# Talking-heads attention and mixture of experts: all four batches in float32, v as the stationary operand, products ordered by array form

## The chip, the cores and the metric

One NeuronCore of a Trainium2 chip. The metric is device microseconds of one execution; lower is better. The profile is of one execution of the program, taken by the hardware profiler. The engines are TensorE (PE; its weight loads PEld), VectorE (DVE), ScalarE (ACT), GpSimd (POOL) and SyncE (SP), which issues most DMAs.

## What is computed

Attention over 4 batches, 12 heads, 448 rows, head size 64, with the heads mixed by a 12 x 12 matrix before the softmax and by another after it; then each of the 1792 rows (12 heads x 64 = 768 values) goes through one of 8 experts, chosen by the largest cosine logit.

```python
scores = scale * np.matmul(q, k.transpose(0, 1, 3, 2))
scores = np.einsum('bhij,hg->bgij', scores, w_pre)
attn = exp(scores - max); attn = attn / (sum + 1e-9)
attn = np.einsum('bhij,hg->bgij', attn, w_post)
x = np.matmul(attn, v)              # 1792 rows of 768
e = argmax(normed(x) @ normed(expert_emb).T / tau)
out = gate * (relu(x @ w1[e]) @ w2[e])
```

## The kernel before

**Row tiles and groups.** A batch's 448 rows are cut into four row tiles of 110, 110, 110 and 120 rows, 16 in all. A row tile is worked through in groups of 10 rows: 10 rows x 12 heads fill 120 partitions, so that the mixing of heads is a product with a 120-row block matrix. There are 11 or 12 groups in a row tile, 180 in the program.

**One row tile.** `emit_qk` (`emit_qk32` in batch 0) makes the scores of two heads at a time into the PSUM tiles p_s; they are copied to SBUF (shl) and written to a DRAM tile `sdr`. `emit_read` reads them back in three chunks of up to four groups with the rows regrouped (g). For each group `emit_pre` mixes the heads (p_p), `emit_max` takes the row maxima, `emit_exp` the exponentials and their sums, `emit_r` the reciprocal and, on GpSimd, the post-mixing matrix scaled by it (wr); `emit_post` mixes the heads and turns the result at once (p_m: three products of 128 columns of e, and two halves of 64 for the rest), and it is copied into a whole row tile of attention weights. `emit_av` multiplies them with v for the row tile before; `emit_xc`, `emit_xt`, `emit_xtc`, `emit_lg` copy x, turn it, and take the eight logits. x goes to the DRAM tensor x_tok, from which the experts' part gathers rows.

**Two number formats.** In batch 0 scores and pre-mixing are float32; a head's scores come from a q tile whose other 64 rows are zeros, so that all 128 rows of the array are used for one head. In batches 1 to 3 q, k, the scores and w_pre are pairs of float16 pieces (hi and lo): `prep(b)` loads the batch's q, k and v twice, once for the largest magnitude and once for the pieces; `pow2` takes the maximum over the partitions with GpSimd's partition_all_reduce and forms powers of two from it; ScalarE makes the hi pieces, GpSimd or VectorE the lo pieces, and `stack` copies q and k pieces from SBUF to SBUF so that the two pieces lie in the two halves of the partitions. In all batches the attention weights (ahi, alo) and v (vh, vl) are float16 pieces, and `emit_av` takes three products for each of four key blocks of a head, with the weights stationary (128 x 128) and 64 columns of v moving.

**What sets the order.** Every engine's program is in the order in which the code emits it. The main loop runs over the 180 groups; `PLAN` and the lists MX1, MX2, ST1 and others give the group of the row tile in which each piece of side work is emitted. Within a turn gi of the loop: reciprocal of gi - 1, the copies left from the turn before (late_a, late_v), exponential of gi, pre-mixing of gi + 2, scores of a later row tile, post-mixing of gi - 2, logits, transposes, products with v, reads, maxima of gi + 2, prepared parts. Scores run about one row tile ahead. `s_p` has 2 buffers of three heads' score pieces, `g_p` 4 chunks. PSUM: two banks for p_s, three for p_p, two for p_m, one (xb) for x, its transposes and logits. At the start the first row tile's scores go from SBUF straight into `g_first`, without DRAM.

The functions that the change touches:

Of the kernel before, what the change touches and what calls it, by code (L numbers as in the profile page):

```python
# [26 lines left out]
AW = 42 * 120  # L27
NTL = 4 * B
NE = 12
CAP = 256  # L30
CCH = 8
MAXO = 12
NRAW = 9
MX1 = (3, 3, 2, 2, 3, 4, 4, 10, 6, 6, 9, 10, 18, 19, 21, 23, 22, 22)
H1 = 14
V0 = 8
HV = 4
VL = 3
ST1 = (8, 15)
ST2 = 13  # L40
RO = 5
MX2 = (-18, -17, -15, -15, -16, -15, -14, -12, -13, -15, -14, -10, -9, -10, -9, -9, -7, -7)
NW = 5
NWARM = 7
SUMS = ((0, 4), (2, 5), (3, 5), (3, 4), (0, 6), (3, 6), (1, 4), (2, 4), (0, 5))
LEAD = 4
RD0 = (4, 5, 6)
RD = (5, 7, 10)
Q0P = (4, 8, 9, 9)
# [5 lines left out]
QPH3 = 10  # L55
NS = 18
TP = 8
QPH = 10
PLAN = {
    "small": {  # L60
        "qk": (0, 2, 4, 6, 8, 10),
        "av": (3, 3, 3, 4, 5, 6, 6, 7, 9, 9, 10, 10),
        "xc": (5, 8, 11),
        "xt": (7, 8, 11),
        "xtc": (8, 11, 13),
        "sq": 13,
        "lg": (8, 12, 13),
    },
    "large": {
        "qk": (0, 2, 4, 8, 9, 10),  # L70
        "av": (2, 3, 3, 3, 5, 5, 6, 8, 10, 10, 10, 10),
        "xc": (5, 9, 11),
        "xt": (5, 9, 13),
        "xtc": (6, 11, 14),
        "sq": 16,
        "lg": (9, 13, 15),
    },
    "ahead": {
        "av": (4, 4, 4, 4, 6, 6, 7, 7, 8, 9, 9, 9),
        "xc": (5, 8, 10),  # L80
        "xt": (7, 9, 10),
        "xtc": (9, 10, 12),
        "sq": 13,
        "lg": (9, 12, 13),
    },
    "last": {
        "av": (2, 2, 3, 3, 4, 4, 5, 5, 6, 6, 6, 7),
        "xc": (4, 6, 8),
        "xt": (4, 7, 8),
        "xtc": (5, 8, 11),  # L90
        "sq": 11,
    },
}
# [5 lines left out]
def talking_heads_moe(  # L99
# [3 lines left out]
    q0: bass.AP,  # L103
# [3 lines left out]
    wpre32: bass.AP,  # L107
# [24 lines left out]
    wpre_sb = const.tile([120, 64], F32, name="wpre_sb")  # L132
    wpre32_sb = const.tile([120, 128], F32, name="wpre32_sb")
# [49 lines left out]
    with tc.manual_schedule():  # L183
# [6 lines left out]
        big = ax.enter_context(tc.tile_pool(name="big", bufs=1))  # L190
        g_p = ax.enter_context(tc.tile_pool(name="g", bufs=4))
# [10 lines left out]
        def open_tmp():  # L202

            nonlocal tmp_p
            gx.close()
            tmp_p = bx.enter_context(tc.tile_pool(name="tmp", bufs=1, side="right"))
# [649 lines left out]
        for n in range(2, 6):  # L856
            load_k(n)
# [660 lines left out]
```

## Time and profile before

| | us |
|---|---|
| median of 3 runs (1039.89 to 1054.26) | 1046.91 |
| the profiled execution | 1048.54 |
| its span, first to last instruction | 1046.7 |
| TensorE busy, VectorE, ScalarE, GpSimd | 895.5, 612.7, 552.2, 253.7 |
| mean granted TensorE clock, share of 2.4 GHz | 0.902 |
| DMA moved | 189.61 MB |

The sum of busy times says little here, since the program has three stages: the start-up to the first exponential, the 180 groups, and the experts. It is read stage by stage.

### The profile page before, as it was taken

The numbers are of one execution on the slowest core, as the hardware profiler recorded it, in microseconds if no ns is written. First come the engines' busy times: TensorE is split into PE (matmuls) and PEld (weight loads), VectorE is DVE, ScalarE is ACT, GpSimd is POOL, SyncE is SP. The second block draws the span as 40 slices with busy tenths as digits, with TensorE's granted clock in tenths as the row PEclk, the third lists the DMA queues.
The fourth block names the chain that finished last, engine by engine and source line by source line (L and its number), as shares of the span: only waits on it lengthen the run. The fifth ranks groups of instructions, "written<-read, shape, count | busy, mean of one in ns | idle before, by whom it ended". The sixth has DMA issues, their size and how long they took to land. (4 is left out here: it accounts for less than half of the span.)

```text
span 1046.7 us, 20350 instructions
## 1 busy us (share of the span) xinstructions
PE 895.5 (86%) x7532; PEld 690.9 (66%) x7532; DVE 612.7 (59%) x1559; ACT 552.2 (53%) x1168; POOL 253.7 (24%) x526
## 2 busy tenths in 40 slices
PE   7295969849979586989999989897799999999995
PEld 3162746526645454656666656676699999999994
DVE  1063546536876353768657767465467865565562
ACT  4073745526857263867657756463254543454351
POOL 3021423003533111545112212223142012111110
PEclk9597988878989696999989989798999999999998
DMA  8785785855878655668756655722587667765671
GB/s 156 156 212 154 210 253 141 221 132 169 231 209 246 180 99 130 198 190 241 213 109 186 188 146 110 226 74 81 86 298 227 222 197 225 238 213 194 196 244 45
DMA packets 99246, 189.61 MB, mean 181 GB/s; under 512 B 9809, under 2 KB 68377, under 8 KB 99144
## 3 DMA queue, kind: packets, MB, share of 16 engines
q1 hardware_dynamic: 95591, 175.75, 61.1%
q0 software_dynamic: 3552, 12.53, 3.6%
q8 instruction: 60, 0.98, 0.4%
q14 instruction: 43, 0.34, 0.1%
HBM read 130.27 MB, written 48.54 MB: 171 GB/s over the span
## 5 line engine op out<-in xcount | busy, mean ns | idle before, releaser
L621 PEld LDWEIGHTS p_m<-wr,e 128*128 128x128 f32 x1080 | 152.1, 210 | 112.3 <-POOL wr L612 62.1
L621 PE MATMUL p_m<-wr,e 128*128 128x120 f32 x1080 | 181.2, 309 | 51.0 <-POOL wr L612 51.0
L632 ACT ACTIVATE ahi<-p_m 128x420 f16<-128x420 f32 x180 | 97.9, 544 | 126.1 <-PE p_m L623 125.1
L635 DVE TENSOR_TENSOR alo<-p_m,ahi 128x420 f16<-128x420 f32 x180 | 106.3, 590 | 97.1 <-ACT ahi L632 96.5
L612 POOL TENSOR_TENSOR wr<-wpost_sb,r 128x120 f32<-128x120 f32 x180 | 69.9, 388 | 373.1 <-DVE r L609 279.4
L592 DVE TENSOR_REDUCE mn<-p_p 128x1 f32<-128x448 f32 x180 | 110.1, 612 | 69.0 <-PE p_p L583 43.2
L954 ACT ACTIVATE wh<-raw_w 128x768 fp32r<-128x768 f32 (+2 forms) x132 | 113.1, 903 | 45.3 <-DMA raw_w<-w 37.6
L955 DVE TENSOR_TENSOR wl<-raw_w,wh 128x768 fp32r<-128x768 f32 (+2 forms) x128 | 126.9, 1030 | 15.4 <-ACT wh L954 15.3
L523 DVE SCALAR_TENSOR_TENSOR shl<-p_s,shl 110x448 f16<-110x448 f32 (+1 forms) x144 | 83.3, 617 | 53.6 <-ACT shl L520 53.4
L520 ACT ACTIVATE shl<-p_s 110x448 f16<-110x448 f32 (+1 forms) x144 | 70.9, 542 | 74.8 <-DMA sdr<-shl 38.3
L600 ACT ACTIVATE e<-p_p,mn,uo 128x448 f32<-128x448 f32 x135 | 97.7, 724 | 0.0
L651 PEld LDWEIGHTS <-ahi 128*128 128x128 f16 (+1 forms) x1536 | 87.9, 101 | 13.6
L1304 PE MATMUL p_h<-xh,wh 128*128 128x256 f32 x336 | 96.8, 288 | 0.0
L1304 PE MATMUL p_h<-xh,wl 128*128 128x256 f32 x336 | 95.1, 283 | 0.0
L1304 PE MATMUL p_h<-xl,wh 128*128 128x256 f32 x336 | 95.1, 283 | 0.0
L651 PE MATMUL xb<-vh,ahi 128*128 128x64 f16 x720 | 94.0, 201 | 0.0
L651 PE MATMUL xb<-vh,alo 128*128 128x64 f16 x720 | 93.3, 198 | 0.0
L651 PE MATMUL xb<-vl,ahi 128*128 128x64 f16 x720 | 93.3, 198 | 0.0
L1056 POOL DMA_INDIRECT out<-o,idx_s x17 | 23.6, 1388 | 218.6 <-DVE o L1324 183.4
L1322 PE MATMUL p_o<-wh,hh 128*128 128x384 f32 x224 | 75.6, 338 | 0.0
L1306 ACT ACTIVATE hh<-p_h 128x512 fp32r<-128x512 f32 x28 | 16.7, 598 | 111.2 <-PE p_h L1304 91.6
L1322 PE MATMUL p_o<-wl,hh 128*128 128x384 f32 x224 | 74.9, 334 | 0.0
(269 smaller groups left out, 1898.2 us busy)
## 6 DMA issues: line engine op xcount, KB each, us to landing
g<-sdr SPq DMA_DIRECT2D x34, 840.0 KB
raw_w<-w SPq DMA_DIRECT2D x54, 512.0 KB
raw_w<-w SPq DMA_DIRECT2D x72, 384.0 KB
sdr<-shl SPq DMA_DIRECT2D x42, 577.5 KB
sdr<-shl SPq DMA_DIRECT2D x16, 630.0 KB
raw<-vP SPq DMA_DIRECT2D x36, 256.0 KB
raw<-qT SPq DMA_DIRECT2D x36, 224.0 KB
raw<-kT SPq DMA_DIRECT2D x36, 224.0 KB
```

The source lines that it names most:

```text
L520: A.activation(out=sb[:n, j, :], in_=p[:n, :S], func=ACTF.Copy, scale=2.0 ** -19)
L523: V.scalar_tensor_tensor(out=sb[:n, j + 1, :], in0=p[:n, :S], scalar=2.0 ** -19, in1=sb[:n, j, :], op0=ALU.mult, op1=ALU.subtract)
L592: V.tensor_reduce(out=mn[:, 0:1], in_=p[:, :S], op=ALU.max, axis=AX.X, negate=True)
L600: A.activation(out=e, in_=p[:, :S], func=ACTF.Exp, scale=exp_scale(gi)[:, 0:1], bias=mn[:, 0:1], accum_out=mn[:, 1:2])
L621: T.matmul(p[:, jt * 120:jt * 120 + 120], e[:, jt * 128:jt * 128 + 128], wr, start=True, stop=True)
L632: A.activation(out=dst(ahi), in_=src, func=ACTF.Copy)
L635: V.tensor_tensor(out=dst(alo), in0=src, in1=dst(ahi), op=ALU.subtract)
L651: T.matmul(p[:, g % 4 * D:(g % 4 + 1) * D], a[t % 2][r, a0:a0 + 128], v[r, c0:c0 + D], start=(jt == 0 and k == 0), stop=(jt == 3 and k == 2))
L954: A.activation(out=h[:, c], in_=r[:, c], func=ACTF.Copy)
L955: lo = lambda: eng.tensor_tensor(out=l[:, c], in0=r[:, c], in1=h[:, c].bitcast(F32), op=ALU.subtract)
L1304: T.matmul(p[:, f], lt[:, c], rt_[:, k], start=(k == 0 and i == 0), stop=(k == KD - 1 and i == 2))
L1322: T.matmul(p[:, :384], lt[:, k, c], rt_[:, m], start=(k == 0 and i == 0), stop=(k == KF - 1 and i == 2))
```

## The change

The float16 pieces, `prep`, `pow2` and the lists that placed them are gone. All batches go the way of batch 0, in float32, with these differences. The scores of two heads come from rows 0 to 63 and 64 to 127 of q and k as they are loaded (no zeros), into two PSUM banks. The first row tile's scores go through DRAM too. All score copies of the loop are on VectorE, all copies of p_m on ScalarE. In `emit_av` v is stationary: for a pair of heads, one product of 128 x 128 and six of 128 x 64, whose results lie turned (features on partitions), so the copy of that gives the logits' operand, and x is turned back by transposes. In a turn the products stand in the order of their form: pre-mixing, transposes, logits, first part of post-mixing, first product with v (128 x 128); second part of post-mixing and the six products with v (128 rows x 64 columns); scores (64 rows x 128 columns).

```diff
-        def prep(b):
...
-        def pow2(mx, n, top, tag):
...
-            G_.partition_all_reduce(out_ap=ar, in_ap=mx, channels=128, reduce_op=bass_isa.ReduceOp.max)
...
+        qk_p = bx.enter_context(tc.tile_pool(name="qk", bufs=2, side="right"))
+        s_p = bx.enter_context(tc.tile_pool(name="s", bufs=6, side="right"))
...
+        def emit_qk(t, a, banks, engs):
...
+            for u in range(2):
+                own = slice(64 * u, 64 * u + 64)
+                T.matmul(ps[u][:n, :S], q_sb[b][own, a, c0:c0 + n], k_sb[b][own, a, :], start=True, stop=True)
...
+                    if engs[u] is A:
+                        A.activation(out=sb[:n, u], in_=ps[u][:n, :S], func=ACTF.Copy, scale=0.125)
                     else:
...
+                        V.tensor_scalar(out=sb[:n, u], in0=ps[u][:n, :S], scalar1=0.125, scalar2=None, op0=ALU.mult)
+                qk_done[0] += 1
+                Y.dma_start(out=sdr[t][2 * a:2 * a + 2].rearrange("h i s -> i h s"), in_=sb[:n])
...
-            for w, st_, sp_ in ((wh, True, False), (wl, False, True)) if t > 3 else ():
-                for u in range(2):
-                    T.matmul(p[64 * u:64 * u + 64, :S], w, gt[t, 2 * m // CCH][:, 2 * m % CCH + u, :], start=st_, stop=sp_)
+            T.matmul(p[:, :S], wpre_sb, gt[t, m // CCH][:, m % CCH, :], start=True, stop=True)
...
-            G_.tensor_tensor(out=mn[:, 0:1], in0=mn[:, 0:1], in1=exp_scale(gi), op=ALU.mult)
...
-                V.tensor_tensor(out=dst(alo), in0=src, in1=dst(ahi), op=ALU.subtract)
...
+        def emit_av(t, a, p=None, c=None):
...
+            T.matmul(p[:, c:c + n], v[:, 768 + v0:768 + v0 + 128], w[:, (36 + a) * 120:(36 + a) * 120 + n],
+                     start=True, stop=False, skip_group_check=True)
+            yield
+            for jt in range(3):
+                for u in range(2):
+                    x0 = (jt * H + a + 6 * u) * 120
+                    d0 = jt * 256 + v0 + 64 * u
+                    T.matmul(p[64 * u:64 * u + 64, c:c + n], v[:, d0:d0 + 64], w[:, x0:x0 + n],
+                             start=False, stop=(jt == 2), skip_group_check=True)
+            yield
...
+        for ch in range(3):
+            emit_read(0, ch)
+        for j in range(3):
+            load_v(0, j)
...
+            for f in halves:
+                next(f)
+
+            want = min(6 * NTL, 6 * (t + 1) + QPH // 2 + sum(q <= pos for q in QK_AT))
+            if qk_n < want:
+                tq, a = divmod(qk_n, 6)
+                late_v.append(emit_qk(tq, a, banks[:2], (V, V)))
```

How the order moves, on TensorE in the middle of a batch: before, from the last pre-mixing product of a turn (p_p) over the scores of two heads (p_s) and the post-mixing (p_m) to the first products with v (xb); an x and a number counts products that follow each other.

```order
L586 LDWEIGHTS wl
L586 MATMUL p_p<-g,wl 64x448
L511 LDWEIGHTS qs
L511 MATMUL p_s<-kh,qs 110x448
...
L514 LDWEIGHTS qs
L514 MATMUL p_s<-tl,qs 110x448
...
L621 MATMUL p_m<-wr,e 128x120 x3
L623 MATMUL p_m<-wr,e 64x60 x2
L651 LDWEIGHTS ahi_132
L651 MATMUL xb<-vh,ahi_132 128x64
L651 LDWEIGHTS alo_134
L651 MATMUL xb<-vh,alo_134 128x64
```

And now, a whole turn of row tile 1 and the head of the next, which has a pair of transposes (L354):

```order
L270 MATMUL p_p<-g,wpre_sb 128x448
L303 MATMUL p_m<-wr,e 128x120 x3
L327 MATMUL xb<-att_126,v 128x110
L306 MATMUL p_m<-wr,e 64x60 x2
L334 MATMUL xb<-att_126,v 64x110 x6
L240 MATMUL p_s<-k,q 120x448 x2
L270 MATMUL p_p<-g,wpre_sb 128x448
L354 MATMUL xb<-id_sb,xT 110x128 x2
```

What moved: the scores stand behind everything else of the turn, the two parts of post-mixing are pulled apart by the first product with v, and twelve products with v for each head have become seven for a pair.

On GpSimd in row tile 2, before: the scaled post-mixing matrix (wr) of each group, the scaling of the maxima (mn), the lo pieces (tt, tl), and between them the maximum over partitions (p2r) with an instruction (ISA) ahead of it and one behind it.

```order
L612 TENSOR_TENSOR wr<-wpost_sb,r 128x120
L593 TENSOR_TENSOR mn<-mn,u_raw 128x1
L412 TENSOR_TENSOR tt<-raw,p2s 128x448
L211 ISA
L211 ISA p2r<-m_1268 128x1
L612 ISA
L612 TENSOR_TENSOR wr<-wpost_sb,r 128x120
L593 TENSOR_TENSOR mn<-mn,u_raw 128x1
L414 TENSOR_TENSOR tl<-tt,th 128x448
```

And now, GpSimd from the end of the start-up on; x156 are the matrices wr of the first 156 groups:

```order
L174 DMA id_sb<-ident 128x128
L175 DMA valid_sb<-valid 128x16
L176 DMA tokid_sb<-tokid 128x16
L177 DMA tri_sb<-tri 128x128
L293 TENSOR_TENSOR wr<-wpost_sb,r 128x120 x156
L493 MEMSET pre 128x8
```

What moved: nothing is left on GpSimd between the matrices of the groups.

On SyncE at the start, before: loads, twelve copies of the first scores into g (L550), and two writes of row tile 1's scores.

```order
L851 DMA qs<-kT 128x448 x2
L851 DMA kh<-kT 128x448 x3
L860 DMA qs<-q 64x6x230
L860 DMA kh<-q 64x6x230
L550 DMA g_130<-alo_133 10x11x448 x6
L550 DMA g_130<-ahi_131 10x11x448 x6
L552 DMA sdr_243<-alo_134 110x3x448 x2
```

And now:

```order
L215 DMA q<-qT 128x6x110
L221 DMA k<-kT 128x448 x6
L215 DMA q<-qT 128x6x340
L250 DMA sdr<-s_sb 110x2x448 x6
L260 DMA g<-sdr 120x1792 x2
L260 DMA g<-sdr 120x1344
L226 DMA v<-vP 128x1024 x3
```

What moved: the copies into g have become six writes to DRAM (L250) and three reads behind them (L260), and one load of q stands ahead of the writes.

## Rows read from the trace of the kernel before

**Rows 1.** Busy time of each engine by stretch, with the counts of instructions; the last three columns are the granted clock (1.00 is 2.4 GHz), the busy share of the DMA engines and what they moved in GB/s. The stretches run from the first exponential of one row tile to the first of another: the start-up, row tiles 0 and 3 (float32), 4, 6 and 8 (float16 pieces), and all that follows the last exponential.

```profile
0.00:49.40 49.40, 21.75 (x54) 11.20 (x55) 5.03 (x18) 11.06 (x20) 8.60 (x19) 0.77 0.80 152
49.40:86.90 37.50, 31.65 (x150) 18.81 (x149) 23.19 (x83) 24.16 (x59) 7.26 (x30) 0.96 0.80 227
...
181.80:248.90 67.10, 47.91 (x346) 30.37 (x345) 28.18 (x83) 28.57 (x70) 7.55 (x26) 0.77 0.59 158
248.90:280.60 31.70, 30.91 (x343) 20.64 (x342) 28.27 (x70) 27.16 (x65) 17.68 (x33) 1.00 0.87 250
...
321.40:369.90 48.50, 35.40 (x342) 23.92 (x340) 24.53 (x83) 24.98 (x65) 8.46 (x26) 0.79 0.66 187
...
422.20:453.00 30.80, 30.80 (x342) 20.63 (x342) 24.61 (x65) 27.23 (x65) 17.95 (x34) 1.00 0.81 230
...
698.40:1046.70 348.30, 322.60 (x2282) 312.17 (x2281) 205.77 (x358) 143.63 (x207) 68.30 (x61) 0.97 0.60 186
```

**Rows 2.** Who waited for whom over the whole program: microseconds in total, times, longest.

```profile
PE p_m L621 <- POOL wr L612: 51.0, 7, 13.1
...
POOL wr L612 <- issue: 42.9, 7, 10.6
...
ACT shl L520 <- DMA sdr<-shl: 38.3, 14, 6.7
```

**Rows 3.** GpSimd's instructions in order of time, from 335 to 353 us (start, duration, line, in brackets the idle time before it).

```profile
339.94 0.37 POOL L211 PARTITION_ALL_REDUCE p2r<-m  x1 [5.95 <-issue]
350.86 0.38 POOL L612 TENSOR_TENSOR wr<-wpost_sb,r 128x120 f32<-128x120 f32 x1 [10.55 <-issue]
```

**Rows 4.** TensorE in the same view, from 347 to 351.6 us.

```profile
351.30 0.57 PE L621 MATMUL p_m<-wr,e 128*128 128x120 f32 x1 [13.05 <-POOL wr L612]
```

**Rows 5.** SyncE's DMA issues from 8 to 36 us; a merged row gives the first start, the time from there to the end of the last issue, and the count.

```profile
14.59 12.49 SPq L550 DMA_DIRECT2D g<-ahi  x6
28.64 2.68 SPq L552 DMA_DIRECT2D sdr<-alo  x2
33.09 0.37 SPq L338 DMA_DIRECT2D raw<-qT  x1
```

**Rows 6.** TensorE from 32 to 53 us.

```profile
46.59 4.42 PE L583 MATMUL p_p<-g,wpre_sb 120*128 120x448 f32 x6 [24.88 <-DMA sdr<-alo]
```

**Rows 7.** ScalarE from 49 to 50 us.

```profile
49.40 0.72 ACT L600 ACTIVATE e<-p_p,mn,u_raw 128x448 f32<-128x448 f32 x1 [27.10 <-POOL mn L593]
```

**Rows 8.** TensorE from 64 to 73 us, row tile 0, all in float32. A float32 product shows as two records, so x2 on L583 is one product, x6 on L621 three, x4 on L623 two, and x2 on each row of L539 one.

```profile
65.86 0.83 PE L621 MATMUL p_m<-wr,e 128*128 128x120 f32 x6
66.62 0.33 PE L623 MATMUL p_m<-wr,e 128*64 128x60 f32 x4
66.88 1.02 PE L583 MATMUL p_p<-g,wpre_sb 120*128 120x448 f32 x2
67.74 0.83 PE L621 MATMUL p_m<-wr,e 128*128 128x120 f32 x6
...
69.61 0.92 PE L539 MATMUL p_s<-qs 128*110 128x448 f32 x2
...
71.12 0.82 PE L621 MATMUL p_m<-wr,e 128*128 128x120 f32 x6
```

**Rows 9.** TensorE from 432 to 441 us, row tile 8, float16 pieces. L586 is pre-mixing, L511 and L514 are the scores of two heads, L651 the products with v of one head (twelve records, of which the first stands here).

```profile
432.13 0.38 PE L586 MATMUL p_p<-g,wh 120*64 120x448 f16 x2
...
432.63 0.58 PE L511 MATMUL p_s<-kh,qs 128*110 128x448 f16 x2
433.14 0.40 PE L514 MATMUL p_s<-tl,qs 64*110 64x448 f16 x2
433.47 0.93 PE L621 MATMUL p_m<-wr,e 128*128 128x120 f32 x6
...
434.59 0.20 PE L651 MATMUL xb<-vh,ahi 128*128 128x64 f16 x1
...
435.05 0.38 PE L586 MATMUL p_p<-g,wh 120*64 120x448 f16 x2
```

**Rows 10.** TensorE's weight loads from 438.2 to 440 us, same view.

```profile
438.56 0.74 PEld L621 LDWEIGHTS p_m<-wr,e 128*128 128x128 f32 x6 [0.20 <-POOL wr L612]
439.42 0.20 PEld L623 LDWEIGHTS p_m<-wr,e 128*64 128x64 f32 x4
```

**Rows 11.** TensorE from 425 to 426.3 us: logits (L693, two products) and transposes (L678, two).

```profile
425.58 0.55 PE L693 MATMUL xb<-enT,xT 128*110 128x8 f32 x4
425.99 0.39 PE L678 MATMUL xb<-id_sb,xs 110*128 110x110 f32 x2
```

**Rows 12.** Groups of instructions of row tile 8 (422.2 to 453 us): line, engine, operation, names, shapes, count, then busy us and mean ns of one, then idle time before them.

```profile
L600 ACT ACTIVATE e<-p_p,mn,uo 128x448 f32<-128x448 f32 x12 | 8.7, 728 | 0.0
...
L592 DVE TENSOR_REDUCE mn<-p_p 128x1 f32<-128x448 f32 x12 | 7.3, 607 | 0.4 <-PE p_p L586 0.3
...
L523 DVE SCALAR_TENSOR_TENSOR shl<-p_s,shl 110x448 f16<-110x448 f32 x12 | 6.9, 618 | 3.2 <-ACT shl L520 3.2
L632 ACT ACTIVATE ahi<-p_m 128x420 f16<-128x420 f32 x12 | 6.6, 548 | 2.5 <-PE p_m L623 2.5
```

**Rows 13.** DMA issues by what they write and read: count and KB each.

```profile
raw<-qT SPq DMA_DIRECT2D x36, 224.0 KB
...
kh<-th SPq DMA_DIRECT2D x24, 168.0 KB
```

More of the change, by code (lines that the diff above doesn't have):

```diff
@@ L54 @@
 SA = (1, 2, 0, 1, 0, 1, 3, 3)
[L55 to L93, printed above, removed]
+AV_AT = (2, 3, 4, 5, 6, 7)
+XTC_AT = (4, 6, 8)
+XT_AT = (5, 7, 9)
+XC_AT = (6, 8, 10)
+LG_AT = 9
+SQ_AT = 11
+LOADS = (0, 1, 2, 3, 4, 5)
 NSLOT = E * 2 + MAXO
@@ new lines, in talking_heads_moe, with load_q, load_k, load_v @@
+        q_sb, k_sb, v_sb = {}, {}, {}
+        def load_q(b, c, w):
+            if b not in q_sb:
+                q_sb[b] = qk_p.tile([128, H // 2, NQ], F32, tag="q", name="q")
+            Y.dma_start(out=q_sb[b][:, :, c:c + w], in_=qT[b, :, :, c:c + w])
+        def load_k(b, a, n):
+            if b not in k_sb:
+                k_sb[b] = qk_p.tile([128, H // 2, S], F32, tag="k", name="k")
+            Y.dma_start(out=k_sb[b][:, a:a + n], in_=kT[b, :, a:a + n])
+        def load_v(b, j):
+            v_sb[b, j] = v_p.tile([128, 1024], F32, tag="v", name="v")
+            Y.dma_start(out=v_sb[b, j], in_=vP[b, :, j * 1024:j * 1024 + 1024])
@@ new lines, in emit_av, with emit_xtc @@
+            yield
+        def emit_xtc(t, k, p=None, eng=None):
+            n = SIZES[t % 4]
+            p = xb if p is None else p
+            if k == 0:
+                xT_sb[t] = x_p.tile([128, KD, 120], F32, tag="xT", name="xT")
+            src = p[:, :240].rearrange("p (k i) -> p k i", i=120)[:, :, :n]
+            dst = xT_sb[t][:, 2 * k:2 * k + 2, :n]
+            if eng is V:
+                V.tensor_copy(out=dst, in_=src)
+            else:
+                A.activation(out=dst, in_=src, func=ACTF.Copy)
@@ L655, in emit_xc, with emit_xt @@
+        def emit_xt(t, k, p=None, c=256):
+            p = xb if p is None else p
+            n = SIZES[t % 4]
+            for kk in range(2):
+                T.transpose(p[:n, c + kk * 128:c + kk * 128 + 128], xT_sb[t][:, 2 * k + kk, :n], id_sb)
+        def emit_xc(t, k, p=None, c=256):
             p = xb if p is None else p
@@ L892, in talking_heads_moe @@
-        av_pos, x_a, x_t, x_l = {}, {}, {}, {}
+            f0 = first[4 * b - 3]
+            for i in range(6):
+                bg_at(f0 + i, lambda b=b, i=i: load_k(b, i, 1))
+            for i, (c, w) in enumerate(((0, QS[2]), (QS[2], NQ - QS[2]))):
+                bg_at(f0 + 6 + i, lambda b=b, c=c, w=w: load_q(b, c, w))
+            for j in range(3):
+                bg_at(first[4 * b] + (0, 4, 6)[j], lambda b=b, j=j: load_v(b, j))
+        av_at, x_a, x_t, x_l = {}, {}, {}, {}
         for t in range(1, NTL):
@@ L1145, in talking_heads_moe @@
+            for a in av_at.pop(gi, ()):
+                av = emit_av(*a)
+                next(av)
+                halves.append(av)
+            for f in halves:
[4 more added lines that the diff above has]
+                late_v.append(emit_qk(tq, a, banks[:2], (V, V)))
+                qk_n += 1
+            assert gi < p_open or qk_n == 6 * NTL
             if t + 1 < NTL:
```

577 lines of the change are left out of this document (107 added, 470 removed).

## Prediction

> **What bounds the kernel now.** I read the busy times by stage first, since the page's sums mix three stages [rows 1]. The start-up takes 49.4 us, the 180 groups run from 49.40 [rows 7] to the last exponential at 698.4, that is 649 us, and the experts' part takes 348.3 us. The third stage is untouched but for its first products; the other two are where the change acts.
>
> In the middle stage the row tiles differ widely. Row tiles 4 and 8 take 31.7 and 30.8 us with TensorE busy 30.9 and 30.8 us at full clock: there TensorE is the bound. Row tile 6, with the same products, takes 48.5 us at a mean clock of 0.79, and row tile 3 takes 67.1 us at 0.77 [rows 1]. So the second question is what stops TensorE there. The waits say: 51.0 us in seven waits of up to 13.1 us for wr, which GpSimd makes, and GpSimd's own 42.9 us in seven waits of up to 10.6 us with "issue" as the releaser, that is with nothing to wait for [rows 2]. Followed in time, one of the seven is a partition_all_reduce at 339.94, 5.95 us after GpSimd's last work, and the next wr comes 10.55 us after it [rows 3]; TensorE stands still for 13.05 us and goes on when that wr is done [rows 4]. GpSimd is idle most of the time, yet it sets the end in those stretches. A second stall is ScalarE waiting 38.3 us in 14 waits for score buffers whose writes to DRAM have not landed [rows 2], behind the loads and copies of the prepared parts on SyncE's queue.
>
> The start-up is bound by DMA: the engines are 0.80 busy and yet move 152 GB/s only [rows 1]. Six copies of 192.5 KB into g take 12.49 us to issue, some 92 GB/s, where two writes of 577.5 KB to DRAM pass in 33.09 - 28.64 = 4.45 us, 260 GB/s [rows 5]. TensorE waits for this 24.88 us until 46.59 [rows 6].
>
> **The change part by part.** Prices on TensorE are differences of starts at full clock, so that loads of weights and changes of array form are in them. First a test of the method on row tile 8 [rows 9, 11]: pre-mixing 432.63 - 432.13 = 0.50, post-mixing 434.59 - 433.47 = 1.12, scores of two heads 433.47 - 432.63 = 0.84, products with v of a head 435.05 - 434.59 = 0.46, a logits product or a transpose about 0.2. That makes 11 x 1.62 + 6 x 0.84 + 12 x 0.46 + 12 x 0.2 = 30.8 us, and the row tile took 30.8 [rows 1].
>
> *A group in float32* costs 67.74 - 65.86 = 1.88 us for pre- and post-mixing, and row tile 0 does run groups at this pace, so the chain of maximum, exponential, reciprocal and wr can follow it [rows 8]. 180 x 1.88 = 338 us.
>
> *Scores.* One float32 pass of 448 columns takes (71.12 - 69.61) / 4 = 0.378 us [rows 8], and a head needs two. The two heads now lie in different halves of the rows. The trace shows no such pair in float32. The nearest row is L514, the float16 pair on 64 rows each: both pass in 433.47 - 433.14 = 0.33 us, where one stream of 448 float16 columns is half a float32 pass, 0.19, so the two run side by side and 0.14 is the change of form [rows 9]. I take 2 x 0.378 + 0.14 = 0.90; the upper bound is one after the other, 4 x 0.378 + 0.14 = 1.65, as the zero-padded heads of row tile 0 do. 90 pairs in the stage: 81 us, at most 149.
>
> *Products with v.* For a pair of heads two passes of 128 x 128 and, of the six 128 x 64 products, three pairs of two passes side by side, as the four records of L623 do in 66.88 - 66.62 = 0.26 us for 60 columns [rows 8]. A pass of 120 columns costs (66.62 - 65.86) / 6 = 0.127 us with its change of form. So 8 x 0.127 = 1.02 us, against 0.92 for two heads before; 90 pairs: 92 us. This charges the change of form for each run of six passes, some 10 us too much over the stage, and I leave it there for small waits on g that the trace before has too.
>
> *Logits and transposes* 12 x 0.2 = 2.4 us for a row tile as before, 15 times: 36 us. The stage on TensorE: 338 + 81 + 92 + 36 = 547 us against 649.
>
> The Trainium skill, "TensorE: Matmul & The Clock Gate", Part 3 (packing small matmuls), says that a weight load overlaps products in flight only where the row groups differ; all products with v use all rows, so by it their loads would stand in line. The trace does not bear this out: six loads of 128 columns take 0.74 us [rows 10] within the 0.76 us of their six products.
>
> *What goes.* All partition_all_reduces go, and with them the seven waits of 51.0 us together [rows 2] and the lowered clock around them. GpSimd keeps one wr for each group. The 36 loads of 224 KB of q, 24 copies of k between the halves [rows 13] and the like for k, v and q shrink to one load of each for a batch; SyncE's queue holds little but score writes, reads and x, and the score copies have 12 heads of buffers instead of 6. So the releasers of both stalls are gone, not moved.
>
> *What is late next.* ScalarE for a row tile of 11 groups: 11 x (0.73 + 0.55) and some 6 us for reading the sums and for x, 20 us; VectorE: 11 x 0.61 + 12 x 0.62 and some 3 us for reciprocals, 17 us [rows 12]; TensorE: 11 x 1.88 + 6 x 0.90 + 6 x 1.02 + 2.4 = 34.6. Both others are covered. DMA moves some 6.2 MB for a row tile, 25 us at the 250 GB/s of row tile 4 [rows 1]. All-float32 costs about 3.8 us more for a row tile than the undisturbed 30.8, and wins by what no longer stands still.
>
> *Start-up.* The first scores now go through DRAM. Until the first chunk lands 0.34 + 1.38 + 1.04 MB of q and k, 2.37 MB of scores and 0.86 MB of the chunk must pass, 6.0 MB in order on one queue: 24 us at 250 GB/s, 39 us at the 152 GB/s of the old start-up [rows 1]. I take 30, nearer to the fast row since the slow copies into g are gone, but above it for the read that must wait until the last write has landed; and 2.8 us from the first product on g to the first exponential (46.59 to 49.40) [rows 6, 7]: 33 us against 49.4, bounds 27 and 42.
>
> *Tail.* The last row tile's products with v cost 6.1 us instead of 5.5 and one batch of logits moves into the loop; 347 instead of 348.3.
>
> **The sum.** 33 + 547 + 347 = 927 us of span. The profiled execution had 1.8 us outside its span and lay 1.6 us above the median, so 927 against the median of 1046.91, 11% less.
>
> **Rivals.** *Float32 pairs in row halves run one after the other.* Speaks for it that no row shows them; against it the float16 pair. 90 x 0.75 = 68 us more: 995.
>
> *Loads of weights in the narrow form stand in line.* 0.05 us for a load (0.20 / 4) [rows 10], six passes a pair: 90 x 0.3 = 27 us more, 954. The page named above would have it so; the row speaks against it.
>
> *Each row tile waits for its scores.* A chunk is read back behind the writes on SyncE's queue. If a read is late in all 15 row tiles by 6.7 us, the longest wait for a landed write [rows 2], it is 100 us and the gain is given back: 1027. Against it: reads are issued five groups, some 15 us, ahead, and in row tiles 4 and 8 the same distance sufficed at a DMA share of 0.81 to 0.87 [rows 1].
>
> *Slower: narrow forms give float32 nothing at all.* If neither halves of rows nor halves of columns overlap and loads stand in line, a pair's scores cost 0.75 us more and its products with v twelve passes of 0.127 + 0.05 instead of six of 0.127, 1.36 more: 90 x 2.1 = 190 us, 1117. It turns slower where the two together exceed 1.3 us for a pair of heads. The four L623 records in 0.26 us speak against it.
>
> **How the numbers follow.** Forecast 0.73 (905 to 960: start-up from 27 to 42, TensorE's stage 3% either way); loads in line 0.08; row halves in turn 0.10; late chunks 0.05; slower 0.03; the rest is faster than the forecast's own range. The range 895 to 980 takes in the first two and the cheap side and leaves out 0.18. About 2% is what a measurement of this kernel tells from no change: faster than 1026 has 0.92, within 2% 0.05, slower 0.03.
>
> **What would show it.** In the changed trace: no GpSimd idle time with "issue" ahead of wr; score pairs whose records start within some ns of each other and a turn without scores and v at 1.88 us; row tiles between 33 and 37 us, all alike, at a clock near 1.00 from row tile 1 on; first exponential near 33 us. It is wrong if score records of two heads follow each other by 0.75 us, if VectorE's score copy waits for landed writes, or if TensorE waits for g at each row tile's start.

## The result and the profile after

The changed kernel takes 914.14 us (907.74 to 922.87, four executions) against 1043.40 us (1038.43 to 1054.26, four) beside it: ratio 0.876, 95% interval 0.865 to 0.886, some 129 us less. Timed again in the last experiment it took 911.06 us, ratio 0.873 (0.868 to 0.878). The forecast was 927, the range 895 to 980. The profiled execution took 907.74 us with a span of 905.9 and 1.8 us outside it. Ratios are of the executions in the fast state alone; the highest of both ranges here, and one execution each of two experiments below (4018.62 and 1685.53 us), were slow.

From the page of the changed kernel: its busy times, the granted clock in 40 slices and the bytes moved:

```profile
PE 855.5 (94%) x6302; PEld 670.6 (74%) x6302; DVE 477.3 (53%) x1262; ACT 407.9 (45%) x887; POOL 146.5 (16%) x267
...
PEclk8799999999999999999999999897999999999997
...
DMA packets 66300, 170.50 MB, mean 188 GB/s; under 512 B 8864, under 2 KB 38944, under 8 KB 66216
```

By stretches, the answer to [rows 1]: the start-up up to the first exponential, row tiles 1, 3 and 8, and from the last exponential to the end. Columns: length, busy time of each engine with its instructions, granted clock, DMA share, GB/s.

```profile
0.00:30.55 30.55, 12.57 (x42) 7.34 (x43) 4.71 (x11) 4.55 (x8) 5.10 (x14) 0.76 0.78 239
...
63.80:97.40 33.60, 33.60 (x263) 22.53 (x260) 15.49 (x47) 15.51 (x42) 4.25 (x11) 1.00 0.88 270
130.20:165.10 34.90, 34.90 (x272) 23.65 (x271) 16.86 (x52) 17.34 (x46) 4.88 (x13) 1.00 0.52 163
298.60:331.60 33.00, 33.00 (x259) 22.30 (x258) 14.38 (x44) 15.72 (x42) 4.02 (x11) 1.00 0.65 190
...
557.73:905.90 348.17, 320.13 (x2204) 309.65 (x2203) 203.39 (x352) 144.17 (x208) 68.40 (x60) 0.96 0.60 186
```

In row tiles 1 to 14, of which three stand here, TensorE is busy without a gap and at full clock. Row tile 3, which took 67.1 us [rows 1], takes 34.9 (it has twelve groups; up to row tile 13 a tile of eleven takes 32.8 to 33.6). From the first to the last exponential, which starts at 557.73, it is 527.2 us instead of 649; the start-up is 18.9 us shorter, the tail is as it was. What TensorE still waits for, the answer to [rows 2]:

```profile
PE p_p L270 <- DMA g<-sdr: 18.0, 2, 16.0
...
PE p_m L303 <- POOL wr L293: 2.0, 1, 2.0
```

The 51.0 us for wr in seven waits are 2.0 in one, at the last group. Of the 18.0 for g the start-up has 16.0; the waits left out here are those of the routing and experts' part. TensorE's own records in row tile 5, the answer to [rows 8, 9] (L270 pre-mixes, L303 and L306 post-mix, L327 and L334 are the products with v, L240 the scores):

```profile
200.49 1.02 PE L270 MATMUL p_p<-g,wpre_sb 120*128 120x448 f32 x2
201.34 0.83 PE L303 MATMUL p_m<-wr,e 128*128 128x120 f32 x6
202.10 0.33 PE L306 MATMUL p_m<-wr,e 128*64 128x60 f32 x4
202.36 1.02 PE L270 MATMUL p_p<-g,wpre_sb 120*128 120x448 f32 x2
203.22 0.83 PE L303 MATMUL p_m<-wr,e 128*128 128x120 f32 x6
203.88 0.38 PE L327 MATMUL xb<-att,v 128*128 128x110 f32 x2
204.19 0.33 PE L306 MATMUL p_m<-wr,e 128*64 128x60 f32 x4
204.35 0.74 PE L334 MATMUL xb<-att,v 128*64 128x110 f32 x12
205.02 1.02 PE L240 MATMUL p_s<-k,q 64*120 64x448 f32 x4
205.97 1.02 PE L270 MATMUL p_p<-g,wpre_sb 120*128 120x448 f32 x2
```

A bare group is 202.36 - 200.49 = 1.87 us. The next turn has a pair of heads' products with v as well: 205.02 - 202.36 = 2.66, so they add 0.79. A pair of heads' scores takes 205.97 - 205.02 = 0.95.

### The profile page after: what moved, and what is told of

Read it like the earlier page. It is cut to its first block, busy times and chain, and to the rows that moved or that the text cites. A ratio compares the mean times of both kernels' runs of the same rounds, so it can differ in the third digit from the quotient of the medians.

```text
span 905.9 us, 16962 instructions
## 1 busy us (share of the span) xinstructions
PE 855.5 (94%) x6302; PEld 670.6 (74%) x6302; DVE 477.3 (53%) x1262; ACT 407.9 (45%) x887; POOL 146.5 (16%) x267
## 5 line engine op out<-in xcount | busy, mean ns | idle before, releaser
L312 ACT ACTIVATE att<-p_m 128x420 f32<-128x420 f32 x180 | 107.9, 599 | 263.9 <-PE p_m L306 263.7
L270 PE MATMUL p_p<-g,wpre_sb 120*128 120x448 f32 x360 | 185.0, 597 | 18.4 <-DMA g<-sdr 18.0
L303 PEld LDWEIGHTS p_m<-wr,e 128*128 128x128 f32 x1080 | 145.4, 192 | 51.0 <-issue 46.9
L248 DVE TENSOR_SCALAR s_sb<-p_s 110x448 f32<-110x448 f32 (+1 forms) x186 | 107.8, 620 | 124.2 <-PE p_s L240 121.9
L303 PE MATMUL p_m<-wr,e 128*128 128x120 f32 x1080 | 150.0, 275 | 2.0 <-POOL wr L293 2.0
L621 DVE TENSOR_TENSOR wl<-raw_w,wh 128x768 fp32r<-128x768 f32 (+2 forms) x128 | 127.3, 1032 | 14.9 <-ACT wh L620 14.8
L282 ACT ACTIVATE e<-p_p,mn 128x448 f32<-128x448 f32 x180 | 112.6, 626 | 18.7 <-DVE mn L275 18.7
L270 PEld LDWEIGHTS p_p<-g,wpre_sb 120*128 120x128 f32 x360 | 54.5, 190 | 89.4 <-ACT att L312 32.6
L240 PE MATMUL p_s<-k,q 64*110 64x448 f32 (+1 forms) x384 | 98.3, 591 | 1.0 <-DMA k<-kT 1.0
L965 PE MATMUL p_o<-wh,hl 128*128 128x384 f32 x224 | 74.9, 334 | 0.0
L334 PE MATMUL xb<-att,v 128*64 128x110 f32 (+1 forms) x1080 | 67.6, 260 | 0.0
L947 PEld LDWEIGHTS p_h<-xl,wh 128*128 128x128 f32 x336 | 64.4, 192 | 0.0
L947 PEld LDWEIGHTS p_h<-xh,wh 128*128 128x128 f32 x336 | 64.4, 192 | 0.0
```

The costliest lines, as they stand in the source:

```text
L240: T.matmul(ps[u][:n, :S], q_sb[b][own, a, c0:c0 + n], k_sb[b][own, a, :], start=True, stop=True)
L248: V.tensor_scalar(out=sb[:n, u], in0=ps[u][:n, :S], scalar1=0.125, scalar2=None, op0=ALU.mult)
L270: T.matmul(p[:, :S], wpre_sb, gt[t, m // CCH][:, m % CCH, :], start=True, stop=True)
L282: A.activation(out=e, in_=p[:, :S], func=ACTF.Exp, bias=mn[:, 0:1], accum_out=mn[:, 1:2])
L303: T.matmul(p[:, jt * 120:jt * 120 + 120], e[:, jt * 128:jt * 128 + 128], wr, start=True, stop=True)
L312: A.activation(out=dst, in_=src, func=ACTF.Copy)
```

## The experiments

The theory on record: the gain is the standstill that the prepared parts caused, first the all-reduces on GpSimd, then the traffic on SyncE's queue; the products themselves cost a little more than before, and stay that cheap only since narrow products run side by side and stand in order of the array's form.

**The all-reduces alone, taken from the kernel before.** The scale is a constant instead of the maximum over all partitions; all else stays.

```diff
-            G_.partition_all_reduce(out_ap=ar, in_ap=mx, channels=128, reduce_op=bass_isa.ReduceOp.max)
+            V.tensor_scalar(out=ar, in0=mx, scalar1=0.0, scalar2=8.0, op0=ALU.mult, op1=ALU.add)
```

> The kernel before, with the maximum over the partitions left out: a constant 8 stands in its place, made on VectorE, so GpSimd has no partition_all_reduce; all pieces, loads and copies of the prepared parts stay. Theory (GpSimd stands still around each partition_all_reduce and TensorE with it): the seven waits of 51.0 us go and about 20 us of lowered clock with them, the 649 us between first and last exponential become about 575, the time about 970 instead of 1043. Rival (the stalls belong to the volume or the order of the prepared parts' DMAs, and wr is only where they show): the waits move to another releaser and the time stays within 2% of 1043.

986.46 us (982.38 to 991.79), ratio 0.948 (0.941 to 0.954): 54 us less than before. From the first to the last exponential it is 586.0 us. TensorE's waits in this kernel:

```profile
PE p_p L586 <- ACT e L600: 21.4, 6, 5.8
PE p_p L586 <- DMA g<-sdr: 7.5, 3, 3.5
...
PE p_s L511 <- DMA kh<-th: 5.6, 2, 4.5
...
PE p_m L621 <- POOL wr L612: 2.7, 2, 2.3
```

And ScalarE's for landed score writes, 38.3 us in 14 before [rows 2]:

```profile
ACT shl L520 <- DMA sdr<-shl: 34.7, 12, 7.5
```

The waits for wr are gone and the second kind shows: ScalarE still waits for score buffers, is late with e behind its score copies, and chunks and copies of k land late. So the all-reduces are some 54 of the 129 us, and in the profiled executions 63 of the 122 us that the stage gains (649 to 586.0 and 527.2).

**The all-reduces alone, added to the changed kernel.** Seven of them, on a constant tile that nothing reads, in the row tiles where the kernel before stalled.

```diff
+        for t, o in ((1, 1), (1, 1), (2, 4), (3, 5), (3, 8), (6, 6), (7, 7)):
+            bg_at(first[t] + o, all_reduce)
```

> The changed kernel with seven partition_all_reduces of a 128 x 2 tile put back on GpSimd at the groups where the kernel before has them; nothing reads their result. Theory: each stops GpSimd for some 16 us, of which two turns (some 6 us) are covered, and TensorE's clock falls with it: the 527 us between the exponentials become 585 to 600, the time 970 to 990. Rival (an all-reduce alone costs its 0.37 us, the long idle times around it came from what the kernel before had beside it): within 1% of 914.

976.77 us (974.87 to 988.01), 63 us more than the changed kernel. GpSimd and TensorE around the one in row tile 6:

```profile
295.39 0.39 POOL L293 TENSOR_TENSOR wr<-wpost_sb,r 128x120 f32<-128x120 f32 x1 [0.88 <-DVE r L290]
304.11 0.37 POOL L568 PARTITION_ALL_REDUCE ar<-pz  x1 [8.33 <-DVE r L288]
312.26 0.73 POOL L293 TENSOR_TENSOR wr<-wpost_sb,r 128x120 f32<-128x120 f32 x2 [7.79 <-issue]
```

```profile
301.98 1.02 PE L270 MATMUL p_p<-g,wpre_sb 120*128 120x448 f32 x2
312.70 1.64 PE L303 MATMUL p_m<-wr,e 128*128 128x120 f32 x6 [9.69 <-POOL wr L293]
314.26 0.48 PE L306 MATMUL p_m<-wr,e 128*64 128x60 f32 x4
```

The granted clock behind the wait (last columns as in [rows 1]), and GpSimd's and TensorE's waits in the whole kernel (total, times, longest):

```profile
312.70:314.67 1.97, 1.97 (x10) 1.65 (x11) 0.00 (x0) 0.00 (x0) 0.29 (x1) 0.50 0.00 0
```

```profile
POOL wr L293 <- issue: 48.8, 6, 10.0
PE p_m L303 <- POOL wr L293: 57.5, 7, 12.7
```

From 295.78 to 312.26 GpSimd does 0.37 us of work, and wr is late by it. TensorE waits 9.69 us, and the six products after it take 314.26 - 312.70 = 1.56 us, about double the 0.76 of row tile 5 of the changed kernel, at a granted clock of 0.50 (1.2 GHz). Row tile 6 takes 44.9 us instead of 32.8 and row tile 8, which has none, 33.0. The same stall appears without any prepared part, so the all-reduce is its cause.

What fills the two idle stretches the profile does not say, but its records of GpSimd's queue show where they begin (count, duration in ns, first and last start in us, from 290 to 320 us):

```profile
L568 POOLq MODIFY_POOL_CONFIG  x2: 11/11/11, 296.0 to 296.0; - x2
L293 POOLq MODIFY_POOL_CONFIG  x2: 82/82/83, 304.4 to 304.5; - x2
```

Such a pair stands ahead of the all-reduce, right behind GpSimd's last work, and another ahead of the next wr. It is so in all six places here and around every all-reduce of the kernel before, at the lines where the order shown with the change has an ISA instruction ahead of it and one behind it; the changed kernel and the kernel before without all-reduces have none in the stage. So the idle time goes with GpSimd's change from one kind of instruction to the other and back, 5.8 to 9.0 us ahead of an all-reduce here and 7.0 to 10.0 behind it, and the two all-reduces that stand together share one.

**More traffic without its work.** Loads like those of the kernel before (36 a batch) and 16 copies between halves, 34 MB in all, on SyncE's queue at the old places; nothing reads them.

```diff
+        for b in range(1, B):
+            for i in range(36):
+                bg_at(first[4 * b - 4] + 2 + i, lambda b=b, i=i: more_load(b, i))
+            for i in range(16):
+                bg_at(first[4 * b - 4] + 8 + 2 * i, lambda i=i: more_copy(i))
```

> The changed kernel with DMAs of the kind and number that the prepared parts had put on SyncE's queue beside its own: 108 loads of 224 or 256 KB from q, k and v and 48 copies of 168 KB between the halves of SBUF, spread over row tiles 0 to 11, into tiles that nothing reads. They wait for no engine. Theory (the second stall of the kernel before came from copies on SyncE that waited for lo pieces, not from volume): within 2% of 914, the row tiles still 33 to 35 us. Rival (volume: 33 MB more make score writes and reads late): 15 us or more, row tiles of 36 us and more, waits of TensorE for g.

953.65 us (948.53 to 960.70), ratio 0.912 (0.907 to 0.918): 40 us more. The rival was right. TensorE's waits for g, and row tiles 6, 7 and 10:

```profile
PE p_p L271 <- DMA g<-sdr: 45.5, 10, 16.0
```

```profile
244.63:285.07 40.44, 36.89 (x259) 25.13 (x258) 16.81 (x60) 15.62 (x45) 4.25 (x11) 0.87 1.01 284
285.07:326.51 41.44, 37.35 (x272) 24.85 (x271) 16.84 (x52) 17.30 (x47) 4.89 (x13) 0.92 0.91 207
399.87:432.96 33.09, 33.09 (x259) 22.32 (x260) 16.90 (x60) 15.64 (x44) 4.25 (x11) 1.00 1.00 272
```

In row tile 6 the DMA engines have no share left (1.01 at 284 GB/s) and the next tile's chunk lands late; TensorE stands for 3.55 us and runs on at a granted clock of 0.50 (1.2 GHz) until 280.65 at least. In the profiled executions the span grows by 53.0 us: the waits for g by 27.5, and TensorE's busy time, for the same 6302 products, by 881.8 - 855.5 = 26.3, at a mean granted clock of 0.947 instead of 0.976. Added to the same kernel, this traffic costs 40 us and the all-reduces 63. A full share alone does not decide where: row tile 10 is at 1.00 and takes 33.1 us, and of the slowed row tiles (2, 6, 7, 9 and 11) two, 2 and 6, have a share of 0.54 in the changed kernel. Nor is it the traffic of the kernel before: with it 204.73 MB are moved, and before it were 189.61 MB, some of which waited for pieces, as these loads do not. What the second stall cost in the kernel before is therefore not measured by this run.

**Order by form.** Each batch of products goes through full array and half columns at once, and not all full-array products of a turn first.

```diff
                 next(po)
-                halves.append(po)
+                next(po)
...
             for a in av_at.pop(gi, ()):
-                av = emit_av(*a)
-                next(av)
-                halves.append(av)
-
-            for f in halves:
-                next(f)
+                for _ in emit_av(*a):
+                    pass
```

> The changed kernel without the order by form: the two parts of post-mixing follow each other, then the seven products with v of a pair of heads. In the 90 turns with products with v TensorE goes to the narrow form and back once more. Theory: a change to the narrow form and back costs 0.35 us in the trace of the changed kernel (0.10 and 0.05 on the way there, 0.10 and 0.10 on the way back), so 90 x 0.35 = 32 us more, 946. Rival: the changes are hidden, or the turns wait for something else that takes them up: 914 within 8 us.

938.40 us (936.56 to 940.95), ratio 0.900 (0.895 to 0.905). Undisturbed row tiles take 34.8 us instead of 32.8, and hold 40 changes of form instead of 28, counted in the trace: 2.0 / 6 = 0.33 us for each turn with products with v, or 0.17 for one change. Row tile 6:

```profile
241.53:276.34 34.81, 34.81 (x259) 23.10 (x258) 16.61 (x60) 15.61 (x45) 4.25 (x11) 1.00 0.51 150
```

The order of the products is worth 24 us of the 129 by the medians, 90 x 0.33 = 30 by the row tiles.

**Scores on the same rows.** The second head of each pair uses the first head's 64 rows, so its scores are a copy of the first's; all shapes stay.

```diff
-                own = slice(64 * u, 64 * u + 64)
+                own = slice(0, 64)
```

> The changed kernel with the scores of both heads of a pair taken from rows 0 to 63 (the odd heads' scores are left out, the even heads' stand in their place), so the two products of a pair cannot lie side by side in the array. The experts that rows choose may differ, so the stretch between the exponentials is compared. Theory: a pair costs four passes of 0.376 us instead of two, 0.75 us more in 90 pairs: 68 us more, 595 instead of 527. Rival (two float32 products in row halves share so much else that little was gained): 527 to 545.

977.38 us (971.26 to 980.07), the stage 596.7 us: 69 more than 527.2. The pair in row tile 9, and what follows it:

```profile
384.09 1.75 PE L240 MATMUL p_s<-k,q 64*110 64x448 f32 x4
385.77 1.02 PE L270 MATMUL p_p<-g,wpre_sb 120*128 120x448 f32 x2
```

1.68 us instead of 0.95. Float32 products in different halves of the rows do run side by side, which no row of the trace before showed.

**The attention weights stationary again, in float32.** Products with v as in the kernel before (64 columns of v stream past 128 x 110 weights), x transposed the other way; nothing split.

```diff
+            for g in (2 * a, 2 * a + 1):
+                for jt in range(4):
+                    v = v_sb[t // 4, g // 4]
...
+                    T.matmul(p[:n, g % 4 * D:(g % 4 + 1) * D], att[t % 2][:, a0:a0 + n], v[:, c0:c0 + D],
+                             start=(jt == 0), stop=(jt == 3))
```

> The changed kernel with the attention weights stationary as before, in float32: for a head four products of 128 x 110 weights with 64 moving columns, x not turned, and turned by transposes for the logits. Theory: a product costs two passes of 0.107 us, set by the load of 110 to 120 columns, so a pair of heads 8 x 2 x 0.107 = 1.7 us instead of 0.82; no narrow form in that part saves nothing, since post-mixing has it anyway: 90 x 0.9 = 80 us more, 995. Rival (v stationary is no gain: loads are hidden or columns set the price, 0.053 us a pass): 914 within 10 us.

981.54 us (979.98 to 990.29), ratio 0.943 (0.936 to 0.949). Row tiles 37.3 us instead of 32.8, 0.75 us more for each pair of heads:

```profile
379.84 1.67 PE L327 MATMUL xb<-v,att 128*110 128x64 f32 x16
381.44 0.33 PE L306 MATMUL p_m<-wr,e 128*64 128x60 f32 x4
```

Sixteen passes take 1.60 us, 0.10 each, with 64 columns streaming. The passes of L303, with 120, take (203.88 - 203.22) / 6 = 0.11 in the changed kernel. So the shorter stream gains next to nothing and the number of passes counts; whether the load of 110 columns of weights sets the 0.10 or something else in a pass was not tried. With v stationary there are eight streams for a pair instead of sixteen.

**The start-up's bytes.** The part of q that only later row tiles need is loaded behind the first read of scores: 1.04 MB less ahead of the first chunk.

```diff
-        load_q(0, w0, NQ - w0)
...
-        for ch in range(3):
+        emit_read(0, 0)
+        load_q(0, w0, NQ - w0)
+        for ch in range(1, 3):
             emit_read(0, ch)
```

> The changed kernel with the load of the other 340 columns of q moved on SyncE's queue from ahead of the first score writes to behind the first read of the scores. Theory (the start-up is bound by bytes in order on one queue): 1.04 MB less ahead of the first chunk, 4 us at 250 GB/s: first exponential at 26.5 instead of 30.55, the time 910. Rival (the start-up is bound by latencies, of the write that must land before the read): first exponential within 1 us of 30.5 and no change.

911.02 to 915.46 us in three executions, ratio 0.873 (0.867 to 0.879): no change. The first exponential starts at 29.98 instead of 30.55, where 1.04 MB at the start-up's 239 GB/s would be 4.4 us. SyncE's issues and TensorE's first product on g in the changed kernel:

```profile
7.96 6.47 SPq L250 DMA_DIRECT2D sdr<-s_sb  x6
21.24 1.24 SPq L260 DMA_DIRECT2D g<-sdr  x3
```

```profile
28.02 4.82 PE L270 MATMUL p_p<-g,wpre_sb 120*128 120x448 f32 x6 [15.96 <-DMA g<-sdr]
```

The last write is issued by 14.43, the read goes out at 21.24 when the writes have landed, and its chunk is there at 28.02: two landings of 6.8 us one behind the other. In the experiment the last write is issued by 15.42, the read at 20.82, and the chunk is there at 27.45, so the bytes of q ahead of them hardly count. How much of a landing is the scores' own bytes was not tried; the DMA engines move 236 GB/s during the first and 196 during the second.

**Two changes of form a turn.** If each change of form costs time, turns should run forwards and backwards by turns: full array, scores, half columns; then half columns, scores, full array. In this first kernel the two orders alternate for all products; in turns that begin with half columns and have transposes the products with v come out incomplete, so x is not the reference's there.

```diff
+            for f in narrow if narrow_next else wide:
+                f()
...
+            for f in wide if narrow_next else narrow:
+                f()
+            if narrow:
+                narrow_next = not narrow_next
```

> The changed kernel with turns alternating: one turn does the 128 x 128 products first and the narrow ones last, the next begins with the narrow ones and ends with the 128 x 128 ones; scores stand between the two. Same products. Theory (in the stretch between the exponentials TensorE's passes and changes of form are all there is): one change there and back of 0.35 us less for two turns, 0.175 us a turn, 180 turns: 31 us less, 883. Rival (a second bound close behind: maxima, exponentials or the copies of p_m come a half turn later now): 905 or more, with waits of TensorE for p_m or p_p buffers.

946.56 to 953.92 us in five executions, but with a tail of 387.9 us, which fits the other x sending rows to other experts; only its stage can be compared: 529.5 us, no gain as a whole. Row tiles 2 and 4, of eleven groups both, and two of TensorE's waits:

```profile
104.67:135.62 30.95, 30.62 (x259) 21.12 (x258) 15.88 (x46) 15.15 (x44) 4.38 (x12) 1.00 0.57 168
170.89:205.41 34.52, 33.07 (x262) 22.85 (x258) 15.00 (x48) 15.76 (x43) 4.24 (x11) 1.00 0.62 184
```

```profile
PE xb L340 <- ACT xT L355: 6.8, 14, 0.6
...
PE p_s L240 <- DVE s_sb L248: 4.0, 10, 1.1
```

Row tiles that begin one way gain some 1.9 us (30.95 against 32.8), the others lose up to 1.6 in waits for copies out of PSUM (34.52 against 33.0, of which TensorE is busy 33.07). Between the half-column products with v and their full-array product stood transposes, which start in the same PSUM bank. The Trainium skill, "PSUM — Partial Sum Buffer", The four PSUM rules, says that a starting product clears the marks of the whole bank in the groups of 32 partitions that it writes, so that a later adding product overwrites. The next kernels, where nothing else starts in the bank in between, have tails of 347.9 and 347.3 us again, which agrees with it.

**The same, with the products with v only in turns that begin with the full array.** Both pairs of a column pair stand in one turn, three times a row tile, and the second pair does not start the bank anew.

```diff
-                     start=True, stop=False, skip_group_check=True)
+                     start=start, stop=False, skip_group_check=True)
...
+            back = t and (gi - first[1]) % 2
+            for f in narrow + score + wide if back else wide + score + narrow if t else wide + narrow + score:
+                f()
```

> Again turns alternate (from tile 1 on): full-array products, scores, half-column products in one turn; half-column products, scores, full-array products in the next. The array's form then changes twice a turn and not three times. The products with v stand only in turns that begin with the full array, both pairs of a column pair in one turn, so that nothing else starts in their PSUM bank between their first product and their last. Theory (a change of form costs what the run without the order showed, 0.34 us for two of them): a turn loses 0.17 us, a tile 11 x 0.17 = 1.8 us (32.8 -> 31.0), the stage about 15 x 1.8 = 27 us, and the time goes from 914 to about 888, with the tail at 348 as in the changed kernel. Rival (with scores and mixed weights at uneven distances TensorE waits for ScalarE's and VectorE's copies out of PSUM, as the tiles of one parity did in the first such run, 34.1 to 35.3 us): half of the tiles or all of them stay at 33 us or more, and the time is 905 to 920.

923.48 us (920.91 to 925.47), ratio 0.882 (0.877 to 0.887). The edit missed half of its aim: in turns that run backwards the post-mixing products kept their old order, so a row tile still has 29 to 35 changes of form, counted in the trace, where the changed kernel has 28 or 30, and TensorE's waits for wr grow from 2.0 us to 6.2.

**The same, with the post-mixing products turned too.** Two turns now hold three changes of form, a row tile 16 to 18.

```diff
-                po = emit_post(posts.pop(0))
-                wide.append(lambda: next(po))
-                narrow.append(lambda: next(po))
+                f, g, h = emit_post(posts.pop(0))
+                wide.append(f)
+                narrow.append(g)
```

> The run before did not do what it says in every second turn: there the products for the mixed weights kept their old order (full array first), so that two turns still held five changes of form, as in the changed kernel. Here they are turned too, and two turns hold three. By the records of that run a change adds 0.09 to 0.10 us to the pass behind it (a first pass of the weights' group 0.48 us behind another form and 0.385 behind its own; a half-column pass 0.20 behind a full one and 0.11 otherwise). Theory: 28 changes in a row tile of 11 turns become about 17, so a tile takes 32.8 - 11 x 0.095 = 31.8 us, the stage 527 - 15 = 512 us and the time is about 899. Rival (two turns' products of one form stand right behind each other, so the mixed weights' column sums and the copies out of PSUM are asked for earlier than their engines have them): what the changes give back is waited for on GpSimd's wr or ScalarE's copies, the tiles stay at 33 to 35 us, and the time is 910 to 930.

898.88 us (895.20 to 903.04), ratio 0.864 (0.860 to 0.868). TensorE in row tile 6 (L309 is a half-column product, L305 a full-array one, L358 transposes), and row tiles 5 and 6:

```profile
235.32 0.28 PE L309 MATMUL p_m<-wr,e 128*64 128x60 f32 x4
235.53 1.02 PE L270 MATMUL p_p<-g,wpre_sb 120*128 120x448 f32 x2
236.38 0.83 PE L305 MATMUL p_m<-wr,e 128*128 128x120 f32 x6
237.05 0.38 PE L358 MATMUL xb<-id_sb,xT 128*110 128x128 f32 x2
237.26 0.92 PE L270 MATMUL p_p<-g,wpre_sb 120*128 120x448 f32 x2
238.02 0.82 PE L305 MATMUL p_m<-wr,e 128*128 128x120 f32 x6
```

```profile
195.07:228.23 33.16, 32.29 (x261) 22.59 (x258) 17.43 (x68) 15.53 (x42) 4.09 (x11) 1.00 0.84 247
228.23:259.33 31.10, 30.77 (x259) 21.39 (x258) 17.30 (x59) 15.69 (x45) 4.39 (x12) 1.00 0.58 170
```

Pre-mixing behind half-column products takes 236.38 - 235.53 = 0.85 us, behind full-array ones 238.02 - 237.26 = 0.76: a change lengthens what stands behind it by 0.09 us. That is not all of its price. What stands ahead of it is longer too: in row tile 5 of the changed kernel L303 takes 202.10 - 201.34 = 0.76 ahead of half columns and 203.88 - 203.22 = 0.66 ahead of full-array products. Where hardly anything waits a row tile gains 32.8 - 31.1 = 1.7 us for 11 changes less, 0.155 each, where 1.0 was expected from 0.095 each; most others gain less, with waits for wr, score copies and e of 0.3 to 1.2 us (2.2, 1.7 and 1.4 us in all). The stage falls from 527.2 to 518.3, 9 us where 15 were expected.

**Both side by side.**

> The changed kernel as it is, timed on one chip with the next run. Theory: 905 to 918, as before; first to last exponential 527 us.

> The version with two changes of form a turn, as in the run before, beside the changed kernel. Theory (28 changes of form in a tile become 17, at 0.095 us; part of it waited for again): 10 to 16 us under the changed kernel's time, no execution of the one as slow as the fastest of the other. Rival (the difference seen before was one of chips): the same time within 5 us.

The changed kernel 911.06 us (904.98 to 916.62), ratio 0.873 (0.868 to 0.878); the version with two changes a turn 896.28 (894.53 to 901.32), ratio 0.860 (0.855 to 0.864). No execution of the one lies within the other's range: 14.8 us or 1.6% less. In the two profiled executions the spans are 909.5 and 899.5 us and the stages 530.2 and 522.3; so the profiles show 10 of the 14.8 us, 8 of them in the stage. The rest is in the choice of the execution: the second kernel's profiled one was its slowest (901.32, 5.0 above its median), the first's lay at its median.

## Why the prediction was right, step by step

Forecast 927, measured 914 and 911. The terms of the sum against the profiled execution:

| term | forecast, us | measured, us |
|---|---|---|
| start-up to the first exponential | 33 | 30.55 |
| stage | 547 | 527.2 |
| of it groups, 180 x 1.88 and 1.87 | 338 | 337 |
| scores, 90 x 0.90 and 0.95 | 81 | 85 |
| products with v, 90 x 1.02 and 0.79 | 92 | 71 |
| logits, transposes, waits (measured: what is left of the stage) | 36 | 34 |
| tail | 347 | 348.2 |

The forecast's own terms give 905 to 952 (start-up 27 to 42, stage 3% either way), not the 905 to 960 that it states beside its chance of 0.73; the result lies in both.

**What bounds the kernel.** Right: TensorE where nothing waits, GpSimd's all-reduce where it does. Removing them alone gave 54 us, adding seven alone cost 63. The forecast priced their waits at 51.0 us and the lowered clock beside.

**The second stall.** Right that it goes; its cause is in part argued. The forecast named score buffers behind loads on SyncE's queue, and ScalarE's waits for them do stay, 34.7 us, when the all-reduces alone go. With 34 MB put back into the changed kernel, which has twice the score buffers, it is the next row tile's chunk that lands late. No run separates the buffers from the traffic in the kernel before.

**Products with v**, the mis-sized term: 0.79 us for a pair, not 1.02. The forecast took 0.127 us for each of eight streams, from six passes of the mixing with a change of form in them [rows 8]. In the order by form a turn changes form as often with these products as without, so they cost little but their streams: (205.02 - 204.35) / 6 = 0.11 each for the half columns, with the change behind them. That is 21 us, as much as the stage's whole miss of 20; the 4 us that the scores cost more are nearly made up by smaller terms. The forecast had seen 10 of the 21 and left them in.

The Trainium skill, "TensorE: Matmul & The Clock Gate", Part 3, lets weight loads overlap products only where row groups differ. All twelve records of L334 use all rows and each has its own load (there are as many loads as products on the page, 6302); their pairs stand 0.11 us apart all the same, where a stream of 110 columns alone is 0.378 x 110 / 448 = 0.09 by [rows 8]. So this trace does not agree, and the rival of 954 us, with 0.05 us for each load, fell with it.

**Scores.** Taken from the float16 pair [rows 9] at 0.90, measured 0.95; the experiment on the same rows gave 1.68 and 69 us, the rival's 68.

**Start-up.** Near in size (33 against 30.55), and by luck, since its reason was not the right one: it had 6 MB in order at 200 GB/s, and 1.04 MB less ahead of the chunk took away 0.57 us instead of 5. What stands there is two landings of 6.8 us, one behind the other. The 260 GB/s that it read for two writes is the pace at which they are issued [rows 5]; in the changed kernel six are issued in 6.47 us, and the last has landed 6.8 us later.

**What was to show it.** The score pair's four records in 0.95 us, groups at 1.87, row tiles of 32.8 to 34.9 at full clock, no waits for wr in the middle: all there. One sign was badly chosen: GpSimd idle with "issue" ahead of wr still occurs, at most 4.3 us in three places, and TensorE does not wait there. The label alone says nothing; the wait for wr on TensorE does, and so do the MODIFY_POOL_CONFIG records on GpSimd's queue.

## What to carry to other kernels

Before splitting float32 into float16 parts, price the whole preparation: here the parts saved some 2 us of TensorE in a row tile (30.8 against 32.8) and cost it 18 us in row tile 6 (48.5 against 30.8) [rows 1], through an engine that was 24% busy and, as far as the runs tell, through DMA traffic and score buffers. Price narrow products as differences of starts in the order that they will stand in, and count changes of array form in a turn as a cost of their own, 0.16 to 0.17 us each here, part of it ahead of the change. A transfer whose result goes out and comes back in costs its two landings, 6.8 us each here, so look there before counting the bytes ahead of it.

## What was not expected of the hardware

- An all-reduce over partitions of 0.37 us keeps GpSimd from its next tensor operation for 8 us (48.8 us in six places, two of the seven standing together), and each time, not the first alone. Up to 9.0 us more stand ahead of it. In the place shown the profile puts these down to VectorE, but the all-reduce reads a constant tile there, and the stretch begins with MODIFY_POOL_CONFIG.
- Half-column float32 passes of 110 columns follow each other at (205.02 - 204.35) / 6 = 0.11 us a pair, while each has its own weights.
- A float32 pass with 64 columns streaming past 110 columns of weights takes 0.10 us, hardly less than one of 120 columns past 128, 0.11.
- A change of array form costs some 0.16 us, and not only behind it: the products ahead of it take 0.10 us longer.
